# A two-layer feed-forward behind a short convolution, on one core: from the 37th group of tokens on, first-layer matmuls of 512 columns that two groups share

## The chip, the core and the metric

One NeuronCore of a Trainium2 chip runs the whole program. Its engines are TensorE (PE, with its weight loads shown apart as PEld), VectorE (DVE), ScalarE (ACT), GpSimd (POOL) and SyncE (SP), which issues most of the transfers. Each engine takes its instructions in the order in which the program lists them. The metric is the device time of one execution in microseconds, as the median of several runs.

## The reference, cut to what matters

The input has 8 sequences of 4224 tokens with 192 features; all of it is float32. Seven weights for each token and head are made by a softmax, and each token becomes the weighted sum of itself and the six tokens before it. Then comes a layer norm, a first layer of 192 to 768 with a ReLU, and a second layer of 768 to 192 whose result is added to the layer's input.

```python
w = softmax(weight_gen)                      # (8, 4224, 8 heads, 7)
y[b, s] = sum over k of w[b, s, :, k] * x_pad[b, s + k]     # per head, 24 features each
mu, var = mean(y), mean((y - mu) ** 2)
xn = (y - mu) / sqrt(var + 1e-6) * g_ln
out = y + maximum(xn @ w_ch1, 0) @ w_ch2     # 192 -> 768 -> 192
```

## The kernel before

**Tiling.** A tile is 128 rows of tokens, 16 stretches of each of the 8 sequences; there are 264 tiles. Four tiles make a group, so there are 66 groups, and TensorE works group by group. Ahead of it, in chunks of 4 or 6 tiles, `softmax` and `conv` make `y` (DVE multiplies at L511, POOL and transfers add), and `norm` makes the normalised tokens in two halves, a high and a low float16 part, which a transfer (`turn`, L652) transposes into a buffer `xT`.

**First layer.** For each group, `products` runs three units. A unit (`unit_products`, L670) covers two of the six 128-row blocks of the hidden layer: for each block 9 terms, each with two matmuls of 64 rows, one in the upper and one in the lower half of the array, that run at the same time into two banks of a PSUM buffer `ph`. Each matmul streams the 256 columns that one group has in such a half, so a unit has 36 matmuls. There are two `ph` buffers. `evict` empties one: ACT writes the ReLU as float16 into `hh` (L685), and DVE then writes the remainder into `hlo` (L687). `hh` and `hlo` have two buffers each, one group to a buffer.

**Second layer.** `half_output` (L721) multiplies a group's hidden values with the two halves of the second weights: 72 matmuls of 192 columns, again two at a time, into the one buffer `po`. It runs twice for each group, `p0` and `p1`; between them the row halves swap banks, behind a small SP instruction called `hop`. After `p1`, `merge` adds the result to `y` on DVE (L773, `f`). The last group goes through `output` (L750).

**Order.** Nothing is scheduled by the compiler. Each operation has a name, and the table `PLACE` gives for each name and count its place in one list of 2392 operations for all engines; the program is written out in that order. So an engine's order is the list's, cut down to that engine. For TensorE it repeats `unit`, `unit`, `p0` of the group before, `unit`, `p1` of the group before. At the start the weights arrive as float64 words, and DVE, ACT and POOL turn them into float16 halves (`from_double`, `w_scale`, `weights`); `w_scale` has a tiny matmul in it (L860), once for each layer. A `wake` (L642) of 11 matmuls comes right before the first unit.

Of the kernel before, what the change touches and what calls it, by code (L numbers as in the profile page):

```python
# [16 lines left out]
P = 128  # L17
ALPHA = 8.0
NT = 4
# [6 lines left out]
HALF = 512  # L26
TINY = struct.unpack("<f", struct.pack("<I", (1023 - 126) << 20))[0]
# [4 lines left out]
    'wload': (3, 9, 33, 42, 82, 86, 121, 257, 191, 373, 568, 527, 770, 1053, 851, 1068, 1156, 1216, 1427, 1301,  # L32
        1465, 1705, 1809),
    'load': (26, 12, 32, 37, 85, 87, 102, 103, 84, 120, 298, 261, 337, 260, 421, 466, 456, 526, 338, 569, 642,
        641, 756, 712, 769, 783, 849, 885, 978, 1067, 979, 1162, 1159, 1163, 1302, 1343, 1368, 1369, 1572, 1426,
        1566, 1569, 1613, 1806, 1768, 1769, 1808, 1938, 1905, 2076, 2134, 2035),
    'w_load': (40, 11, 13, 0, 1, 2),
    'w_load2': (58,),
    'w_as': (67,),
    'w_av': (41, 44, 65, 73),  # L40
    'w_an': (80,),
    'w_cs': (20,),
    'w_cv': (15, 17, 22, 23),
    'w_cn': (45,),
    'w_s1': (81, 88, 97, 104, 112),
    'w_h': (122, 123, 125, 127),
    'w_l': (153, 156),
    'w_m': (190, 193, 195, 192),
    'w_c2s': (71, 124, 146),
    'w_c2v': (72, 74, 76, 78, 91, 105, 130, 135, 137, 139, 161, 163),  # L50
    'w_c2n': (93, 144, 168),
    'w_s2': (169, 171, 182, 184, 212, 206, 207, 213),
    'max': (4, 10, 34, 43, 89, 136, 138, 352, 234, 446, 665, 608, 868, 1070, 935, 1103, 1258, 1261, 1474, 1430,
        1592, 1712, 1837),
    'sub': (5, 18, 51, 110, 111, 203, 320, 431, 551, 653, 750, 844, 967, 1148, 1090, 1243, 1406, 1441, 1581,
        1684, 1812, 1850, 1947),
    'exp': (6, 19, 52, 115, 114, 227, 321, 436, 552, 659, 751, 860, 983, 1166, 1114, 1255, 1418, 1459, 1582,
        1700, 1825, 1875, 1964),
    'sum': (7, 21, 66, 131, 133, 242, 350, 495, 553, 664, 752, 929, 1009, 1168, 1126, 1260, 1431, 1480, 1591,
        1719, 1834, 1907, 1991),  # L60
    'rcp': (8, 25, 70, 141, 175, 293, 384, 505, 573, 689, 802, 930, 1011, 1170, 1197, 1289, 1501, 1500, 1628,
        1720, 1880, 1960, 2043),
    'inv': (14, 29, 77, 162, 221, 324, 471, 545, 655, 746, 879, 947, 1078, 1202, 1259, 1388, 1536, 1540, 1644,
        1754, 1928, 2006, 2044),
    'mul': (16, 31, 90, 185, 315, 416, 525, 639, 742, 831, 933, 1018, 1128, 1231, 1328, 1433, 1537, 1636, 1738,
        1823, 1930, 2039, 2131),
    'keep': (24, 54),
# [16 lines left out]
    'copy': (53, 94, 126),  # L84
    'sums': (55, 57, 96, 99, 142, 140, 176, 177, 244, 246, 247, 255, 291, 295, 332, 326, 367, 396, 401, 397,
# [7 lines left out]
    'squares': (56, 68, 98, 100, 148, 147, 178, 180, 245, 251, 252, 256, 296, 306, 334, 333, 386, 398, 409, 412,  # L93
# [909 lines left out]
```

## Time and profile before

| | us |
|---|---|
| median of 3 runs | 868.77 |
| lowest and highest | 868.34, 869.21 |
| the profiled execution, first to last instruction | 867.2 |
| busy: PE, DVE, ACT, POOL | 823.4, 772.1, 683.7, 679.6 |

The span is the time between the first and the last instruction of one profiled execution; the run's time also holds what lies around it, 1.6 us by the median. Busy time is the time in which an engine has at least one instruction running; two matmuls that run at once count once. In a view of stretches, each row is a piece of the span; in a view in order of time, a bracket at the end of a row gives the idle time before the instruction and what ended it. The chain that ended last is followed back from the last instruction, at each step to what released it.

### The profile page before, as it was taken

What the parts mean: (1) busy time and instruction counts of PE and PEld (TensorE: products, weight loads), DVE (VectorE), ACT (ScalarE), POOL (GpSimd) and SP (SyncE); (2) the same over time, 40 slices, a digit from 0 to 9 for tenths busy, and PEclk for the clock granted to TensorE, in tenths of its full rate; (3) what the DMA queues carried; (4) which work ended last, traced back from release to release, by engine and by line L of the source; (5) the groups of instructions that cost most, each with busy time, mean ns of one, the idle gap of its engine ahead of it and who ended that gap; (6) DMA issues with size and microseconds to landing.
All of it is one profiled execution on the core that took longest, in us unless ns stands there. A gap on an engine that the chain in (4) does not pass through costs nothing.

```text
span 867.2 us, 37431 instructions
## 1 busy us (share of the span) xinstructions
PE 823.4 (95%) x16665; PEld 787.7 (91%) x16665; DVE 772.1 (89%) x796; ACT 683.7 (79%) x1781; POOL 679.6 (78%) x390
## 2 busy tenths in 40 slices
PE   3857999999999999999999999999999999999997
PEld 2526999999999999999999999999989999999997
DVE  6899999999999999999999999999989989874442
ACT  2798898799678889889888789787887888796631
POOL 3399999899889999897887889888976788885100
PEclk9968999999999999999999999999999999999999
DMA  7768868988897958988899698878948569565123
GB/s 193 190 127 166 166 163 184 200 176 180 194 193 151 220 94 188 213 181 180 160 205 195 149 213 175 165 139 187 207 99 200 120 151 190 124 127 106 40 76 110
DMA packets 137465, 140.89 MB, mean 162 GB/s; under 512 B 107479, under 2 KB 109015, under 8 KB 137303
## 3 DMA queue, kind: packets, MB, share of 16 engines
q1 hardware_dynamic: 123175, 88.95, 44.9%
q0 software_dynamic: 13824, 49.55, 29.6%
q8 instruction: 130, 2.13, 1.1%
q14 instruction: 32, 0.26, 0.1%
q10 hardware_dynamic: 304, 0.00, 0.0%
HBM read 36.43 MB, written 25.95 MB: 72 GB/s over the span
## 4 chain that ended last, share of the span: by engine, by line
PE 68%; DVE 9%; issue 2%; DVEq 0%
PE ph L670 34%; PE po L721 34%; DVE pr L511 4%; DVE hlo L687 2%; DVE y L511 1%; DVE y L773 1%; PE ph L750 1%; DVE sm L449 0%; DVE mx L440 0%; DVE wn L465 0%; DVE wn L460 0%; DVE wn L461 0%; DVE wn L459 0%; DVE wn L599 0%; DVE wn L601 0%
## 5 line engine op out<-in xcount | busy, mean ns | idle before, releaser
L514 POOL TENSOR_TENSOR y<-y,pr 128x1152 f32<-128x1152 f32 (+1 forms) x192 | 474.5, 2499 | 39.0 <-DVE pr L511 22.1
L670 PE MATMUL ph<-xT,c_w 64*128 64x256 f16 x7128 | 420.0, 270 | 10.5 <-DVE hlo L687 7.8
L670 PEld LDWEIGHTS <-c_w 64*128 64x128 f16 x7128 | 377.6, 94 | 28.3 <-issue 13.5
L721 PE MATMUL po<-c_w2h,hh 64*128 64x192 f16 x3120 | 392.5, 243 | 1.4 <-issue 1.0
L721 PE MATMUL po<-c_w2h,hlo 64*128 64x192 f16 x3120 | 392.4, 243 | 0.5 <-issue 0.5
L721 PE MATMUL po<-c_w2l,hh 64*128 64x192 f16 x3120 | 392.4, 243 | 0.0
L721 PEld LDWEIGHTS <-hh 64*128 64x128 f16 x6240 | 345.7, 94 | 2.8 <-issue 1.9
L511 DVE TENSOR_TENSOR pr<-x,wn 128x2304 f32<-128x2304 f32 (+1 forms) x150 | 332.5, 2226 | 6.6 <-POOL y L514 1.8
L687 DVE SCALAR_TENSOR_TENSOR hlo<-ph,hh 128x1024 f16<-128x1024 f32 x198 | 239.2, 1219 | 57.2 <-ACT hh L685 56.9
L685 ACT ACTIVATE hh<-ph 128x1024 f16<-128x1024 f32 x198 | 200.3, 1015 | 105.2 <-PE ph L670 101.7
L721 PEld LDWEIGHTS <-hlo 64*128 64x128 f16 x3120 | 225.5, 94 | 0.7 <-issue 0.7
L648 POOL TENSOR_TENSOR hl<-xh,hl 128x768 f16<-128x768 f32 x66 | 115.0, 1748 | 44.5 <-ACT hl L635 33.0
L615 ACT ACTIVATE xh<-y,s 128x192 f32<-128x192 f32 x264 | 125.5, 535 | 16.1 <-DVE s L603 12.5
L569 ACT ACTIVATE junk<-y,s 128x192 f32<-128x192 f32 x264 | 119.6, 453 | 6.9
L517 POOL DMA_DIRECT2D pr<-pr x96 | 94.4, 1082 | 37.3 <-DMA xT<-hl 14.2
L564 ACT ACTIVATE junk<-y 128x192 f32<-128x192 f32 x264 | 95.1, 360 | 13.6 <-POOL y L514 7.2
L773 DVE SCALAR_TENSOR_TENSOR y<-po,c_fs,y 128x768 f32<-128x768 f32 (+1 forms) x80 | 67.9, 860 | 5.4 <-PE po L721 5.4
L511 DVE TENSOR_TENSOR y<-x,wn 128x1152 f32<-128x1152 f32 (+1 forms) x51 | 60.0, 1181 | 0.1
L635 ACT ACTIVATE hl<-xh 128x768 f16<-128x768 f32 x66 | 55.0, 837 | 2.1 <-DMA xT<-hl 1.1
L564 ACT ACTIVATION_READ_ACCUMULATOR junk<-y 128x1 f32 x264 | 49.5, 188 | 0.0
L569 ACT ACTIVATION_READ_ACCUMULATOR junk<-y,s 128x1 f32 x264 | 49.4, 187 | 0.0
L532 PE MATMUL ph<-pr,ident 128*128 128x384 f32 x72 | 27.1, 531 | 16.5 <-DVE pr L511 15.6
(76 smaller groups left out, 298.5 us busy)
## 6 DMA issues: line engine op xcount, KB each, us to landing
pr<-pr POOLq DMA_DIRECT2D x60, 576.0 KB, 7.8
x<-in_x_dram SPq DMA_DIRECT2D x30, 576.0 KB, 6.3
out_dram<-y SPq DMA_DIRECT2D x30, 576.0 KB, 5.2
pr<-pr POOLq DMA_DIRECT2D x36, 384.0 KB, 5.8
x<-in_x_dram SPq DMA_DIRECT2D x20, 384.0 KB, 5.5
out_dram<-y SPq DMA_DIRECT2D x20, 384.0 KB, 5.3
w<-in_weight_gen_dram SPq DMA_DIRECT2D x21, 336.0 KB, 5.8
pr<-in_moe_w_ch_dram SPq DMA_DIRECT2D x1, 1152.0 KB
```

Source lines behind the costliest of these rows:

```text
L511: E.tensor_tensor(out=ov, in0=xv, in1=wv, op=ALU.mult)
L514: Q.tensor_tensor(out=flat(0), in0=flat(0), in1=flat(k), op=ALU.add)
L517: return Q.dma_start(flat(to), flat(k), accum_op=ALU.add, max_dma_last_dim=CHUNK * D * 4)
L564: A.activation(junk, at(y)[:, j, :], AF.Identity, scale=-1.0 / D, accum_out=at(s4)[:, 3, t : t + 1])
L569: A.activation(junk, at(y)[:, j, :], AF.Square, bias=at(s4)[:, 3, t : t + 1], accum_out=at(s4)[:, 0, t : t + 1])
L615: A.activation(paired(xh, t), at(y)[:, i, :].rearrange("p (c q) -> p c q", q=P // 2), AF.Identity, bias=at(s4)[:, 3, g + t : g + t + 1], s ...
L648: lambda xh=xh, hl=hl: Q.tensor_tensor(out=halves(hl, True), in0=pairs(xh), in1=halves(hl, False), op=ALU.subtract),
L670: T_.matmul(ph[:, r, v * 2 * P : (v + 1) * 2 * P], W["w1"][rows, WB[r][c], w, f : f + P], xv[rows, a, c, :, :], start=(v == 0 and k == 0), ...
L685: lambda: A.activation(at(hh)[:, us, :], at(ph), AF.Relu), [ph], [(hh, u)])
L687: lambda: V.scalar_tensor_tensor(out=at(hlo)[:, us, :], in0=at(ph), scalar=0.0, in1=at(hh)[:, us, :], op0=ALU.max, op1=ALU.subtract),
L721: made.append(T_.matmul(at(po)[:, z, e * D : (e + 1) * D], token(b, 2 * z + e, j)[rows], W[w][rows, j, :], start=(ph == 0 and e == 0 and k ...
L773: V.scalar_tensor_tensor(out=ysl, in0=at(po)[:, zs[0] : zs[-1] + 1, : 2 * D], scalar=W["fs"][:, 0:1], in1=ysl, op0=ALU.mult, op1=ALU.add)
```

## The change

- Pairs 18 to 31 of groups (the 37th to the 64th group) take a new path, `wide_unit`. Six wide units do the first layer of a pair: each covers one 128-row block for both groups, with 18 matmuls of 512 columns, where before a pair had six units of 36 matmuls of 256 columns. The other 38 groups keep the narrow units.
- `xT` becomes two buffers of a pair each (before: three of a group). `hh` and `hlo` become one tile each with three interleaved slots a, b and c: even groups use a, odd groups b and c in turn.
- A wide unit is evicted as before, with 1024 elements per row on ACT and on DVE. The sixth one of a pair is evicted in two halves of 512, one for each group.
- TensorE's order for a wide pair: `q0` and `q1` (the first half of the second layer of the pair before's even group, cut into hidden blocks 0 to 4 and 5), wide unit 0, `p1` of that group, wide unit 1, half of `p0` of the odd group, wide unit 2, the other half, wide unit 3, half of `p1`, wide unit 4, the other half, wide unit 5. So one second-layer piece stands between any two wide units.
- The constants `ones` and `ident` move into the space of the second weights, and the float64 words and their float32 forms into `xT` and two slots of `hlo`; the accesses there become rows of 128.
- The table `PLACE` is new for all 2460 operations, those of the start and of the narrow groups too. In it `wake` has place 135 (before 208), the first three units have 176, 195 and 217 (before 209, 210 and 224), the second layer's tiny matmul stands behind the first unit (184; before 169 and ahead of `wake`), and the load of the second weights has place 25, ahead of the load of `x` for the third chunk at 26 (before 58 and 37).

```diff
+NARROW = 18
 PLACE = {
...
+    'q1': (1561, 1616, 1706, 1774, 1841, 1920, 1983, 2047, 2128, 2194, 2258, 2320, 2371, 2417),
...
-    pool("xT", 3, [P, NT * NB, P], F16)
-    pool("hh", 2, [P, NF, NT * P], F16)
-    pool("hlo", 2, [P, NF, NT * P], F16)
+    pool("xT", 2, [P, 2 * NT * NB, P], F16)
+    HID = {q: cp.tile([P, 2 * NF, 3, 2 * P], F16, name=q) for q in ("hh", "hlo")}
+    for q in HID:
+        for i, m in enumerate("bac"):
+            plan.pools[q + m] = [HID[q][:, :, i, :]]
...
+    W = {k: cp.tile([P, NF, D], F16, name="c_" + k) for k in ("w2h", "w2l")}
+    ones, ident = (W[k].rearrange("p j d -> p (j d)").bitcast(F32)[:, :P] for k in ("w2h", "w2l"))
...
-            xh, hl, xT = Buf("xh"), Buf("hl"), Buf("xT")
+            xh, hl = Buf("xh"), Buf("hl")
+            m = (S0 + g) // NT
+            if m % 2 == 0:
+                pairs_.append(Buf("xT"))
+            xT, h = pairs_[m // 2], m % 2 ^ m // 2 % 2
+            pa["xT"][g] = (xT, h)
...
+    def wide_products(gps, j, part):
+        xv = at(gps[0]["xT"][0]).rearrange("p (i a c) q -> p a c i q", a=2, c=NB)
+        ph = at(gps[0]["ph"][j])
+        for k, (a, w, c) in list(enumerate(terms))[part]:
+            for r, rows in enumerate((top, bot)):
+                f = (j * P + (F // 2 if r and c == 2 else 0)) % F
+                T_.matmul(ph[:, r, :], W["w1"][rows, WB[r][c], w, f : f + P], xv[rows, a, c, :, :],
+                          start=k == 0, stop=k == len(terms) - 1)
...
+    def wide_unit(gps, j):
+        if j not in gps[0]["ph"]:
+            wide_part(gps, j, "uw", 1944)
...
+        for a, b in ((0, 2),) if j < NF - 1 else ((gps[0]["xT"][1], gps[0]["xT"][1] + 1), (gps[1]["xT"][1], gps[1]["xT"][1] + 1)):
+            who = [gps[z] for z in order[a:b]]
+            n = (b - a) * 2 * NT * P // 2
+            op("ACT", a_ns(n, 50), ("relu", s), lambda a=a, b=b: A.activation(cells("hh", a, b), sums(a, b), AF.Relu), [ph],
+               [(gp["hh"], j) for gp in who])
+            op("V", v_ns(n, 6), ("hlo", s),
+               lambda a=a, b=b: V.scalar_tensor_tensor(out=cells("hlo", a, b), in0=sums(a, b), scalar=0.0, in1=cells("hh", a, b),
+                                                       op0=ALU.max, op1=ALU.subtract),
+               [ph, *((gp["hh"], j) for gp in who)], [(gp["hlo"], j) for gp in who])
...
-    def half_output(gp, ph, s):
+    def half_output(gp, ph, s, js=range(6), es=range(2)):
...
+    def split_output(gp, s):
+        for js in (range(5), range(5, NF)):
+            half_output(gp, 0, s, js)
...
-    raw = (Buf("hh"), Buf("hh"), Buf("pr"))
+    raw = (Buf("xT"), Buf("xT"), Buf("pr"))
...
-        wac, w2r = Buf("hlo"), Buf("hlo")
+        wac, w2r = Buf("hlob"), Buf("hloc")
...
+            q = "a" if m % 2 == 0 else "cb"[m // 2 % 2]
+            groups.append(dict(hh=Buf("hh" + q), hlo=Buf("hlo" + q), pa=pa, g=g, s=pa["S"] + g, m=m, xT=pa["xT"][g], ph={}))
+    for m in range(0, len(groups), 2):
+        gps = groups[m : m + 2]
+        if NARROW <= m // 2 < len(groups) // 2 - 1:
+            first = m // 2 == NARROW
+            for j in range(NF):
+                if j == 0 and not first:
+                    split_output(ahead, prev["s"])
+                wide_unit(gps, j)
+                if first:
+                    if j in (1, 3):
+                        half_output(prev, j // 2, gps[0]["s"])
+                elif j == 0:
+                    half_output(ahead, 1, prev["s"])
+                elif j < 5:
+                    half_output(prev, (j - 1) // 2, gps[0]["s"], es=((j - 1) % 2,))
+            ahead, prev = gps
+            continue
```

## Rows read from the trace of the kernel before

**Rows 1.** The page: span, and busy time of each engine.
```profile
span 867.2 us, 37431 instructions
PE 823.4 (95%) x16665; PEld 787.7 (91%) x16665; DVE 772.1 (89%) x796; ACT 683.7 (79%) x1781; POOL 679.6 (78%) x390
```

**Rows 2.** Stretches: us, busy of PE, PEld, DVE, ACT, POOL; clock; DMA share, GB/s.
```profile
0.00:12.00 12.00, 0.00 (x0) 0.00 (x0) 5.08 (x17) 4.78 (x11) 3.46 (x10) 1.00 0.74 179
12.00:72.00 60.00, 41.05 (x177) 23.94 (x178) 55.75 (x88) 44.27 (x131) 39.89 (x26) 0.87 0.73 168
82.00:500.00 418.00, 413.21 (x8767) 409.06 (x8763) 408.61 (x400) 355.97 (x942) 375.52 (x216) 1.00 0.84 179
500.00:840.00 340.00, 337.98 (x7187) 325.72 (x7185) 286.31 (x277) 267.50 (x684) 250.83 (x136) 1.00 0.68 143
```

**Rows 3.** The chain that ended last, steady state: start, us, what.
```profile
676.18 2.97 PE po L721 x72
679.15 3.93 PE ph L670 x72
683.08 2.97 PE po L721 x72
686.05 1.97 PE ph L670 x36
```

**Rows 4.** The same chain, its last piece.
```profile
856.81 6.06 PE ph L750 x72
```

**Rows 5.** PE's waits, whole span: us, times, longest.
```profile
PE po L860 <- DVE hlo L846: 10.6, 1, 10.6
PE ph L670 <- DVE hlo L687: 7.8, 7, 5.2
```

**Rows 6.** PE in order of time, 57 to 80 us.
```profile
58.15 1.44 PE L860 MATMUL po<-c_s,ones 128*128 128x1 f32 x6 [10.56 <-DVE hlo L846]
...
59.45 4.66 PE L642 MATMUL ph<-hl 128*128 128x512 f16 x11
...
64.04 4.10 PE L670 MATMUL ph<-xT,c_w 64*128 64x256 f16 x72
73.35 6.08 PE L670 MATMUL ph<-xT,c_w 64*128 64x256 f16 x72 [5.21 <-DVE hlo L687]
```

**Rows 7.** DVE in order of time: a wait, the first eviction, the sixth unit's.
```profile
36.48 1.75 DVE L511 TENSOR_TENSOR pr<-x,wn 128x1536 f32<-128x1536 f32 x1 [1.39 <-PE po L860]
...
72.08 1.22 DVE L687 SCALAR_TENSOR_TENSOR hlo<-ph,hh 128x1024 f16<-128x1024 f32 x1
...
90.04 1.22 DVE L687 SCALAR_TENSOR_TENSOR hlo<-ph,hh 128x1024 f16<-128x1024 f32 x1
```

**Rows 8.** The load of the second weights: issues, KB each.
```profile
pr<-in_moe_w_ch_dram SPq DMA_DIRECT2D x1, 1152.0 KB
```

**Rows 9.** Groups by line and shape: busy us, mean ns, idle before.
```profile
L687 DVE SCALAR_TENSOR_TENSOR hlo<-ph,hh 128x1024 f16<-128x1024 f32 x198 | 239.2, 1219 | 57.2 <-ACT hh L685 56.9
L511 DVE TENSOR_TENSOR pr<-x,wn 128x2304 f32<-128x2304 f32 x90 | 228.4, 2545 | 0.6 <-POOL y L514 0.3
...
L773 DVE SCALAR_TENSOR_TENSOR y<-po,c_fs,y 128x768 f32<-128x768 f32 x50 | 50.5, 1010 | 3.4 <-PE po L721 3.4
...
L511 DVE TENSOR_TENSOR y<-x,wn 128x1152 f32<-128x1152 f32 x30 | 40.4, 1345 | 0.1
...
L449 DVE TENSOR_REDUCE sm<-e 128x96 f32<-128x672 f32 x21 | 17.7, 844 | 0.0
L440 DVE TENSOR_REDUCE mx<-w 128x96 f32<-128x672 f32 x21 | 17.7, 843 | 0.0
L773 DVE SCALAR_TENSOR_TENSOR y<-po,c_fs,y 128x384 f32<-128x384 f32 x30 | 17.4, 610 | 2.0 <-PE po L721 2.0
```

**Rows 10.** ACT, then DVE, in order of time: one unit's eviction.
```profile
602.67 1.03 ACT L685 ACTIVATE hh<-ph 128x1024 f16<-128x1024 f32 x1 [2.13 <-PE ph L670]
...
603.73 1.23 DVE L687 SCALAR_TENSOR_TENSOR hlo<-ph,hh 128x1024 f16<-128x1024 f32 x1 [0.47 <-ACT hh L685]
```

**Rows 11.** A short stretch at the start, columns as in rows 2.
```profile
73.30:77.40 4.10, 4.05 (x40) 3.21 (x41) 3.48 (x5) 1.96 (x4) 4.10 (x3) 0.50 0.66 148
```

More of the change, by code (lines that the diff above doesn't have):

```diff
@@ new lines @@
+    'newton': (82, 124, 175, 198, 286, 291, 350, 426, 501, 575, 651, 721, 817, 919, 1015, 1107, 1199, 1312,
[13 rows of a table added]
+    'wake': (135,),
[4 rows of a table added]
+    'turn': (152, 180, 234, 214, 315, 347, 404, 399, 471, 463, 541, 546, 618, 644, 696, 682, 753, 756, 830,
[21 rows of a table added]
+    'halo': (226, 647, 868, 1205, 1426, 1721, 2169),
+    'unit': (176, 195, 217, 223, 240, 253, 267, 272, 287, 303, 318, 333, 352, 363, 367, 384, 386, 408, 423,
[6 rows of a table added]
+    'relu': (183, 200, 224, 251, 241, 258, 274, 289, 300, 307, 323, 343, 354, 370, 376, 392, 396, 416, 425,
[12 rows of a table added]
@@ L199 @@
+    'hlo': (189, 206, 228, 252, 242, 259, 282, 294, 304, 308, 325, 345, 359, 377, 381, 401, 400, 420, 429,
[16 rows of a table added]
+    'hop': (248, 279, 329, 368, 403, 444, 479, 519, 553, 589, 628, 671, 702, 740, 770, 812, 841, 874, 908,
[26 rows of a table added]
 }
@@ L687, in evict, with wide_part @@
            lambda: V.scalar_tensor_tensor(
-               out=at(hlo)[:, us, :], in0=at(ph), scalar=0.0, in1=at(hh)[:, us, :],
+               out=at(hlo)[:, us, :], in0=sums(), scalar=0.0, in1=at(hh)[:, us, :],
                op0=ALU.max, op1=ALU.subtract),
-           [ph, (hh, u)], [(hlo, u)])
+           [ph, (hh, 2 * u), (hh, 2 * u + 1)], [(hlo, 2 * u), (hlo, 2 * u + 1)])
+    def wide_part(gps, j, key, cost, part=slice(None)):
+        if j not in gps[0]["ph"]:
+            gps[0]["ph"][j] = Buf("ph")
+        s = gps[0]["s"] + j * NT / 3
+        op("PE", cost, (key, s), lambda: wide_products(gps, j, part),
+           [(gp["xT"][0], h) for h, gp in enumerate(gps)] + W1S, [gps[0]["ph"][j], "pe"], lat=420.0)
@@ new lines, in wide_unit, with cells, sums @@
+    def wide_unit(gps, j):
+        if j not in gps[0]["ph"]:
+            wide_part(gps, j, "uw", 1944)
+        else:
+            wide_part(gps, j, "ub", 1296, slice(3, None))
+        ph, s = gps[0]["ph"][j], gps[0]["s"] + j * NT / 3
+        lo = gps[0]["m"] // 2 % 2 ^ 1
+        order = sorted(range(2), key=lambda z: gps[z]["xT"][1])
+        def cells(q, a, b):
+            k = j // 2 * 4 + j % 2
+            return HID[q][:, k : k + 3 : 2, lo + a : lo + b, :].rearrange("p r h x -> p r (h x)")
+        def sums(a, b):
+            return at(ph)[:, :, a * 2 * P : b * 2 * P]
+        for a, b in ((0, 2),) if j < NF - 1 else ((gps[0]["xT"][1], gps[0]["xT"][1] + 1), (gps[1]["xT"][1], gps[1]["xT"][1] + 1)):
[7 more added lines that the diff above has]
+               [ph, *((gp["hh"], j) for gp in who)], [(gp["hlo"], j) for gp in who])
@@ L733, in hop @@
                 tc.add_manual_dep(h.ins, m.ins.name, apart, reason="row halves swap banks")
+        cost, last = 247 * len(js) * len(es), js[-1] == NF - 1 and es[-1] == 1
         if ph == 0:
-            op("PE", 2930, ("p0", s), mm, whole(gp), [(po, 0), (po, 1), "pe"], lat=360.0)
-            op("SP", 60, ("hop", s), hop, [(po, 0)], [(po, "hop")])
-        else:
-            op("PE", 2930, ("p1", s), mm, [*whole(gp), (po, "hop")], [(po, 0), (po, 1), "pe"], lat=360.0)
-            merge(gp, range(NT), s)
+            key = "q0" if js[-1] < NF - 1 else "q1" if js[0] else "p0"
+            op("PE", cost, (key, s), mm, whole(gp, js), [(po, 0), (po, 1), "pe"], lat=360.0)
+            if last:
+                op("SP", 60, ("hop", s), hop, [(po, 0)], [(po, "hop")])
+        else:
+            op("PE", cost, ("p1", s), mm, [*whole(gp, js), (po, "hop")], [(po, 0), (po, 1), "pe"], lat=360.0)
+            if last:
+                merge(gp, range(NT), s)
+    def split_output(gp, s):
+        for js in (range(5), range(5, NF)):
+            half_output(gp, 0, s, js)
     def output(gp, t, s):
@@ L939, in weights @@
            ["w2h", "fs", *wv], ["w2"])
+    pairs_ = []
     todo = list(softs)
@@ L957 @@
         norm(pa)
-    prev = None
+    groups = []
     for pa in parts:
         for g in range(0, pa["n"], NT):
-            prev = dict(hh=Buf("hh"), hlo=Buf("hlo"), pa=pa, g=g, s=pa["S"] + g, xT=pa["xT"][g], ph={}, prev=prev)
-            for u in range(3):
-                products(prev, u)
-                if u and prev["prev"]:
-                    half_output(prev["prev"], u - 1, prev["s"])
+            m = len(groups)
+            q = "a" if m % 2 == 0 else "cb"[m // 2 % 2]
+            groups.append(dict(hh=Buf("hh" + q), hlo=Buf("hlo" + q), pa=pa, g=g, s=pa["S"] + g, m=m, xT=pa["xT"][g], ph={}))
+    prev = None
+    for m in range(0, len(groups), 2):
[15 more added lines that the diff above has]
+            continue
+        if m // 2 == len(groups) // 2 - 1:
+            split_output(ahead, prev["s"])
+        for i, gp in enumerate(gps):
+            tail = i == 0 and m // 2 == len(groups) // 2 - 1
+            for u in range(3):
+                products(gp, u)
+                if tail and u == 0:
+                    half_output(ahead, 1, prev["s"])
+                elif u and prev:
+                    half_output(prev, u - 1, gp["s"])
+            prev = gp
     for t in range(NT):
```

155 lines of the change are left out of this document (74 added, 81 removed), and 245 rows, old and new, of the table PLACE.

## Prediction

> **What bounds the kernel now.** I read the page first: PE is busy for 823 of 867.2 us, DVE for 772 [rows 1]. A share over the whole span says little here, so the stretches came next. Up to 82 us PE often waits (busy for 41.05 of the 60 us from 12 to 72); from 82 to 500 us it is idle for only 418.00 - 413.21 = 4.8 us, and from 500 to 840 us for 2.0 us [rows 2]. DVE is almost as full in the first of these (idle 9.4 us) and has room in the second (idle 53.7 us) [rows 2]. So there are two stages to judge: a start, in which the first units wait for others, and a long stage in which PE sets the pace. The chain that ended last agrees: in the steady state it is PE alone, 2.97 + 3.93 + 2.97 + 1.97 = 11.84 us for a group, without a gap [rows 3], and it ends with PE's last group at 862.9 us, behind which only a merge and the last store come [rows 4]. PE's list of waits shows what is left to win by order alone: 10.6 us before the second layer's tiny matmul and 7.8 us on evictions, of which 5.2 are one wait at 73.35 us [rows 5, 6].
>
> **Part 1, the longer matmuls.** Two units are 72 matmuls of 256 columns, two at a time, in 3.93 us: 109.2 ns for such a couple. A second-layer half is 36 couples of 192 columns in 2.97 us: 82.5 ns [rows 3]. The difference of 64 columns costs 26.7 ns, or 0.417 ns per column; 256 columns are then 106.8 ns, and 2.4 ns of a couple don't depend on its length. No row shows a couple of 512 columns at this clock. From below: nothing is saved, 2 x 109.2 = 218.4 ns. From above: all that doesn't depend on length is gone twice, 213.6 ns. Near the line through the two rows, with one fixed part left, it is 213.6 + 2.4 = 216.0 ns, and I take that. A wide pair has 54 couples in place of 108, so 14 pairs save 14 x 54 x 2.4 = 756 x 2.4 ns = 1.8 us; the bounds are 0 and 3.6 us. The 1512 weight loads that go were not on the path: PEld is idle for 14.3 us from 500 to 840 us, against PE's 2.0 [rows 2].
>
> The Trainium skill (TensorE: Matmul & The Clock Gate, "Wait — 56ns, not 53.3ns?") gives 215.7 ns for 512 columns at 2.4 GHz; by that figure the saving would be 756 x 2.7 ns = 2.0 us, and no run before shows it.
>
> **Part 2, the evictions.** A wide unit leaves 1024 elements per row as before, at 1.03 us on ACT and 1.22 us on DVE [rows 9, 10]. The sixth of a pair is cut in two, which adds the fixed part of one instruction on each engine, 14 times. The two merge shapes bound that on DVE: one of 768 elements takes 1.01 us and one of 384 takes 0.61, so a cut costs 0.21 us [rows 9]. That is 14 x 0.21 = 2.9 us on DVE, and I take the same for ACT, where no row shows such a cut; it is hidden in DVE's 53.7 us and ACT's 72.5 us of idle time in that stretch [rows 2], and would cost 2.9 us without that cover.
>
> **Part 3, less room between PE's pieces.** Before, a merge could take 3.93 us, since two units stand between `p1` and the next `p0` [rows 3]. In a wide pair one unit of 54 couples / 6 = 9 x 216.0 = 1.94 us stands there. A merge needs 1.01 us if DVE is free [rows 9], but DVE takes it in order, behind what the list puts ahead. The tightest place is the end of a pair: wide unit 4, 1.48 us of `p1`, wide unit 5, then `q0`, which needs `po` free. That is 1.48 + 1.94 = 3.42 us for the eviction of unit 4 and the merge. A free eviction shows at 602.67: ACT starts, DVE ends at 603.73 + 1.23 = 604.96, so 2.29 us [rows 10]; with a merge of 1.01 behind it, 3.30 us. It fits by 0.1 us. For the narrow groups there were 6.9 us of room between a group's last unit and the `p0` that reads it (2.97 + 3.93). From below a wide pair waits for nothing; from above it waits behind one convolution multiply, 2.54 us [rows 9], so 14 x 2.54 = 35.6 us. I take what the stretch shows now, 2.0 us for all of it [rows 2], so no change: where the list puts a merge or eviction right behind the matmul that feeds it, PE's order around it repeats, and DVE has 53.7 us to give. Queued behind a late merge on DVE are the next eviction and the convolution; PE waits for the merge through `po` and for the eviction through `ph`.
>
> Ahead of the first wide eviction the new list puts four more multiplies of 2.54 us on DVE and one of 1.35 and three reductions of 0.84 fewer, so 6.3 us more [rows 9]. DVE's idle time from 82 to 500 us, 9.4 us, covers it [rows 2]; without that cover it would come out as up to 6.3 us of PE's time, once.
>
> **Part 4, the start.** In the list before, PE has the second layer's tiny matmul and `wake` ahead of its first unit. The matmul starts at 58.15 after 10.6 us of idle time, `wake` at 59.45, the first unit at 64.04 [rows 5, 6]. In the new list the first unit is behind neither wait, so it can start up to 64.04 - 58.15 = 5.9 us earlier if its weights and tokens are there. But the first unit's gain is not PE's: units three and four start at 73.35 because of DVE's eviction [rows 6, 7]. I counted DVE's operations in both lists. Ahead of the first eviction there are 63 instead of 72; ahead of the sixth unit's there are the same 85. So from there on DVE arrives as before, unless it waits less on the way. It waits 60.00 - 55.75 = 4.25 us from 12 to 72 us [rows 2], of which 1.39 are one wait for PE's first tiny matmul [rows 7]. The gain is at most 4.3 us. The loss: the second weights' 1152 KB now pass the third chunk's tokens on SP's queue [rows 8], and at 179 GB/s as in the first 12 us [rows 2] that is up to 6.6 us later for that chunk's multiplies, less what DVE has to do meanwhile. The early `wake` may leave the clock down for the first units; it stood at 0.50, the level of 1.2 GHz, from 73.3 us, behind the 5.2 us wait, and there two units took 6.08 us and not 3.93 [rows 6, 11]. DVE hides that as well. Between -4.3 and +6.6 I take -0.5: the wait on the first tiny matmul is the likeliest to shrink, and the list of 85 is the same.
>
> **Parts at nothing.** The new `xT`, the moved constants and the accesses in rows of 128 change no operation's count or size; DVE and ACT work on the weights ends before 82 us, so their cost would show in the start, and is inside its bounds. `hop` has one unit between `p0` and `p1` as before (1.94 for 1.97 us); it is an instruction behind transfers on SP's queue, and a wait there would hold PE. The end of the list after the 64th group has the same pieces.
>
> **Sum.** The profiled execution is 867.2 us by span and the median of the runs 868.77, 1.56 us more. Span: 867.2 - 1.8 - 0.5 = 864.9; time: 866.5 us.
>
> **Rivals.** A. The forecast: parts 1 and 4 as taken, 865.0 to 868.0 by the saving's bounds and a little of the start. Chance 0.45.
>
> B. The start gives DVE's 4.3 us: 868.8 - 1.8 - 4.3 = 862.7, or 863.5 with part of it. For it: no tiny matmul ahead of the first unit. Against it: the 85 operations. Chance 0.16.
>
> C. Nothing comes out: waits of 0.13 us per wide pair use up the 1.8 us, or a couple of 512 columns costs two of 256. 868.8 us. For it: 0.1 us of room in part 3. Chance 0.19.
>
> D. Slower: the merge at a wide pair's end comes late. If it starts behind half an eviction, 0.6 us, at each pair, 14 x 0.6 = 8.4 us are lost: 868.8 - 1.8 + 8.4 = 875.4. It decides from (1.8 + 1.7) / 14 = 0.25 us per pair on. For it: one unit where two stood. Against it: DVE is idle for 16% of that stretch [rows 2]. Chance 0.16.
>
> E. A much larger fixed part per matmul, which shorter ones pay and longer ones don't. At 24 ns, ten times what the rows give, 756 couples fewer would save 18.1 us: 850.7. Both rows lie on a line that leaves 2.4 ns [rows 3], so chance 0.02. The Trainium skill (TensorEngine Tiling (Array Packing), "Instruction Overhead") states about 60 cycles per matmul, which is about that size as an estimate; this trace disagrees with it for matmuls that follow each other.
>
> F. The clock falls in the wide stage, because PE pauses more often. One fall costs 6.08 - 3.93 = 2.15 us for two units [rows 3, 6]; at every pair, 14 x 2.15 = 30 us: 897. The granted clock is 1.00 from 82 to 840 us, across the waits there [rows 2]. Chance 0.02. The Trainium skill (TensorE: Matmul & The Clock Gate, "A second HAM failure mode: psum-queue depth-cycling") describes that for matmuls of 512 columns that cycle through PSUM.
>
> **How the numbers follow.** What a measurement here tells from no change is about 0.2%, 1.7 us: faster means under 867.0. A gives 0.29 faster and 0.16 same; with B and E faster is 0.47; with C same is 0.35; D and F make slower 0.18. The range goes from 863.0, which leaves out E and the full gain of B (0.05 together), to 871.5, which leaves out most of D and F (0.15). A's own range is 865.0 to 868.0.
>
> **What would show it.** Right: matmuls of 512 columns at 216 ns per couple, a wide pair's period of 23.5 us and not 23.7, PE idle by about 2 us in the wide stage. Part 4: the sixth unit's eviction ends near 90.04 + 1.22 = 91.3 us, as before [rows 7]. Wrong: PE waits on `y` (L773's successor) or on `hlo` ahead of `q0`, or a granted clock under 1.00 there, or a start that differs by more than 2 us.

## The result and the profile after

The changed kernel takes 876.05 us (median of 4 runs, 874.95 to 877.62), the kernel before 868.56 us beside it. The ratio is 1.0087, with a 95% interval of 1.0072 to 1.0103: slower by 0.9%, where a gain of 0.3% was forecast, and outside the range of 863.0 to 871.5. The profiled execution after has a span of 873.2 us and a time of 874.95 us, so 6.0 us of span more than before [rows 1]; it is the fastest of the four, and the medians lie 7.5 us apart. A ratio here and below is taken over the fast runs beside the kernel before and need not be the quotient of two medians, and it leaves out three slow runs of two of the kernels below (1249.55 to 3074.32 us).

The page after: span, busy times, and the shares of the chain that ended last; then the chain's shares on the page before.

```profile
span 873.2 us, 34411 instructions
...
PE 826.1 (95%) x15153; PEld 717.6 (82%) x15153; DVE 774.2 (89%) x810; ACT 685.1 (78%) x1795; POOL 679.4 (78%) x390
...
PE 45%; DVE 33%; POOL 7%; issue 6%; ACT 6%; DMA 2%; SPq 1%; DVEq 0%; POOLq 0%
```

```profile
PE 68%; DVE 9%; issue 2%; DVEq 0%
```

In the steady state before, the chain was PE alone [rows 3]. Over the whole span DVE had 9% of it, and now it has 33%: PE is waiting for others, and the stretches say where (columns as in rows 2).

```profile
12.00:72.00 60.00, 45.51 (x233) 28.94 (x235) 57.22 (x89) 46.61 (x136) 41.04 (x26) 0.90 0.71 172
82.00:500.00 418.00, 410.12 (x8685) 402.87 (x8682) 409.68 (x399) 356.32 (x943) 378.13 (x217) 1.00 0.84 181
500.00:840.00 340.00, 335.26 (x5608) 252.03 (x5605) 282.86 (x290) 266.96 (x697) 247.00 (x134) 1.00 0.67 143
```

Up to 72 us PE is busier than before, by 4.5 us. From 82 to 500 us it is idle for 7.9 us and not 4.8, and from 500 to 840 us for 4.7 and not 2.0 [rows 2]. The granted clock is 1.00 in both, so it is not the clock. PE's list of waits, whole span (us, times, longest), names what it waits for:

```profile
PE ph L699 <- DVE hlo L720: 12.2, 11, 3.6
PE ph L699 <- ACT junk L582: 5.9, 1, 5.9
PE po L786 <- DVE y L847: 4.5, 7, 1.5
...
PE po L786 <- SPq L797: 1.1, 2, 0.7
PE ph L688 <- DVE hlo L754: 1.1, 1, 1.1
PE ph L688 <- DMA xT<-hl: 0.6, 2, 0.4
```

Before, evictions had 7.8 us of PE's time and the tiny second-layer matmul 10.6 [rows 5]; merges had 0.3 us in one place, and `hop` and the transposes none. Now the merges, L847, have 4.5 us in seven places, and `hop` (L797) and the transposes are on the list.

A pair in the wide stage in which no long wait falls looks as forecast. The chain that ended last, late in the stage:

```profile
807.48 1.94 PE ph L688 x18
809.42 3.02 PE po L786 x72
812.43 1.94 PE ph L688 x18
...
833.00 3.04 PE po L786 x69
```

Nine couples of 512 columns take 1.94 us, 215.8 ns each, and the pair's period is 833.00 - 809.42 = 23.58 us. The Trainium skill (TensorE: Matmul & The Clock Gate, "Wait — 56ns, not 53.3ns?") gives 215.7 ns for such a matmul at 2.4 GHz; the trace agrees.

**Three stretches.** To compare kernels I take from each trace when PE starts its 1st and 7th narrow unit, the unit that opens the 37th group, and the first narrow unit of the last pair of groups. With a wide stage one second-layer half, 2.97 us, is still to be done at that last point, and is added to the third stretch. All in us:

```
                           1st unit  7th unit  7th to 37th group  37th group to last pair
before                       64.04     89.61         409.21              334.16
after                        55.24     89.36         412.46              337.11
old_order_new_buffers        65.02     93.87         407.60              333.73
new_order_then_narrow        56.72     90.91         413.21              335.00
old_order_then_wide          64.85     93.77         415.23              337.27
wide_matmuls_cut             55.70     89.86         412.73              339.78
wide_waits_moved             56.71     90.93         412.76              333.64
old_order_own_w2             64.14     89.11         408.04              333.69
old_order_own_w2_again       63.84     88.72         409.19              332.10
after_own_w2                 55.17     91.29         413.12              337.18
own_w2_waits_moved           56.29     92.89         412.94              334.31
after_own_w2_mended          56.20     90.09         413.22              337.14
old_order_wide_moved         64.63     89.43         409.87              332.29
old_order_wide_moved_cut     64.11     89.03         409.64              336.45
narrow_waits_moved           54.84     89.04         412.18              334.17
```

After against before: -0.25 at the 7th unit, +3.25 up to the 37th group, +2.95 in the wide stage, which is the 6.0 us of span. The first column moves by up to 1.9 us between executions of the same order (54.84 to 56.72), so a difference of 1 us in a single trace is read from the stretches and not from the end.

### The profile page after: what moved, and what is told of

It is laid out like the page before. It is cut to its first block, busy times and chain, and to the rows that moved or that the text cites. A ratio compares the mean times of both kernels' runs of the same rounds, so it can differ in the third digit from the quotient of the medians.

```text
span 873.2 us, 34411 instructions
## 1 busy us (share of the span) xinstructions
PE 826.1 (95%) x15153; PEld 717.6 (82%) x15153; DVE 774.2 (89%) x810; ACT 685.1 (78%) x1795; POOL 679.4 (78%) x390
## 3 DMA queue, kind: packets, MB, share of 16 engines
q8 instruction: 118, 1.93, 0.9%
## 4 chain that ended last, share of the span: by engine, by line
PE 45%; DVE 33%; POOL 7%; issue 6%; ACT 6%; DMA 2%; SPq 1%; DVEq 0%; POOLq 0%
PE po L786 21%; DVE pr L524 15%; PE ph L688 12%; PE ph L699 9%; DVE hlo L720 6%; POOL y L527 5%; DVE y L847 3%; DVE y L524 2%; ACT junk L582 2%; PE ph L545 1%; DVE hlo L754 1%; ACT junk L577 1%; DMA xT<-hl 1%; ACT hh L751 1%; DMA x<-in_x_dram 1%
## 5 line engine op out<-in xcount | busy, mean ns | idle before, releaser
L527 POOL TENSOR_TENSOR y<-y,pr 128x1152 f32<-128x1152 f32 (+1 forms) x192 | 465.7, 2432 | 39.3 <-DVE pr L524 16.6
L786 PEld LDWEIGHTS <-hh 64*128 64x128 f16 x6240 | 304.8, 94 | 26.7 <-issue 9.2
L699 PE MATMUL ph<-xT,c_w 64*128 64x256 f16 x4104 | 245.0, 273 | 18.4 <-DVE hlo L720 12.2
L699 PEld LDWEIGHTS <-c_w 64*128 64x128 f16 x4104 | 221.4, 95 | 28.0 <-issue 14.5
L688 PE MATMUL ph<-xT,c_w 64*128 64x512 f16 x1512 | 177.5, 376 | 1.7 <-DVE hlo L754 1.1
L786 PEld LDWEIGHTS <-hlo 64*128 64x128 f16 x3120 | 172.6, 94 | 0.6 <-DVE hlo L754 0.6
L718 ACT ACTIVATE hh<-ph 128x1024 f16<-128x1024 f32 x114 | 115.3, 1013 | 63.6 <-PE ph L699 60.2
L720 DVE SCALAR_TENSOR_TENSOR hlo<-ph,hh 128x1024 f16<-128x1024 f32 x114 | 138.1, 1218 | 16.4 <-ACT hh L718 14.5
L754 DVE SCALAR_TENSOR_TENSOR hlo<-ph,hh 128x1024 f16<-128x1024 f32 (+1 forms) x98 | 104.7, 1068 | 39.1 <-ACT hh L751 38.5
L688 PEld LDWEIGHTS <-c_w 64*128 64x128 f16 x1512 | 81.1, 94 | 64.9 <-issue 1.2
L751 ACT ACTIVATE hh<-ph 128x1024 f16<-128x1024 f32 (+1 forms) x98 | 87.2, 894 | 57.6 <-PE ph L688 41.1
L577 ACT ACTIVATE junk<-y 128x192 f32<-128x192 f32 x264 | 95.1, 360 | 10.6 <-POOL y L527 3.9
L847 DVE SCALAR_TENSOR_TENSOR y<-po,c_fs,y 128x768 f32<-128x768 f32 (+1 forms) x80 | 67.7, 860 | 14.8 <-PE po L786 14.7
```

What stands on the lines that cost most here:

```text
L527: Q.tensor_tensor(out=flat(0), in0=flat(0), in1=flat(k), op=ALU.add)
L577: A.activation(junk, at(y)[:, j, :], AF.Identity, scale=-1.0 / D, accum_out=at(s4)[:, 3, t : t + 1])
L688: T_.matmul(ph[:, r, :], W["w1"][rows, WB[r][c], w, f : f + P], xv[rows, a, c, :, :], start=k == 0, stop=k == len(terms) - 1)
L699: T_.matmul(ph[:, r, v * 2 * P : (v + 1) * 2 * P], W["w1"][rows, WB[r][c], w, f : f + P], xv[rows, a, c, :, :], start=(v == 0 and k == 0), ...
L718: lambda: A.activation(at(hh)[:, us, :], sums(), AF.Relu), [ph], [(hh, 2 * u), (hh, 2 * u + 1)])
L720: lambda: V.scalar_tensor_tensor(out=at(hlo)[:, us, :], in0=sums(), scalar=0.0, in1=at(hh)[:, us, :], op0=ALU.max, op1=ALU.subtract),
```

## The experiments

My theory after the traces: half the loss is the new order of the narrow groups, half are waits in the wide stage; the longer matmuls save what was forecast, and the buffers cost nothing. Rivals: the buffers and their strides; the long matmuls themselves; one of the two halves alone.

**Old order, new buffers.** All groups narrow, PLACE of the kernel before, everything else as changed but for two conditions that let the last pair take the narrow path:

```diff
-NARROW = 18
+NARROW = 33
-    'unit': (176, 195, 217, 223, ...
+    'unit': (209, 210, 224, 228, ...
```

> All groups narrow, in the order of the kernel before (one transpose of 2392 operations is moved by six places, since the paired buffer is free only then), but with the changed kernel's buffers: paired xT, interleaved first-layer buffers read with strides, constants laid over other tiles. Theory (the loss is half in the new order of the start and the narrow groups, half in waits of the wide stage, and buffers cost nothing): 868.6 us, as before, within 1 us. Rival, layout (strided accesses and shared buffers cost the time): slower, by 3 us or more, up to the whole 7.5 us, so 871.5 to 876.

Measured: 871.26 us, ratio 1.0024 (1.0016 to 1.0033). Neither: 2 us slower by the ratio, all from the start, where the third unit comes at 77.37 us and not at 73.35 [rows 6]. PE, DVE and GpSimd of this kernel in order of time:

```profile
77.37 2.96 PE L692 MATMUL ph<-xT,c_w 64*128 64x256 f16 x26 [7.86 <-DVE hlo L713]
...
76.09 1.23 DVE L713 SCALAR_TENSOR_TENSOR hlo<-ph,hh 128x1024 f16<-128x1024 f32 x1 [3.15 <-ACT hl L645]
...
73.10 2.96 POOL L1006 TENSOR_TENSOR c_w2l<-hlo,c_w2h 128x1152 f16<-128x1152 f32 x1
```

The first eviction (L713) stands idle for 3.15 us; the row names an operation of ACT, but it carries a wait on GpSimd's semaphore too, and it starts when GpSimd's L1006 ends, at 73.10 + 2.96 = 76.06. L1006 reads the float32 copy of the second weights. In the changed layout that copy lies in one third of the interleaved `hlo` tile, and the eviction writes another third of it. No cell is shared, but the one waits for the other. From the 7th unit on this kernel is no slower than before (407.60 and 333.73).

**That wait taken away.** The copy goes into a `y` buffer; with it one convolution step that needs such a buffer (`c2` of the ninth chunk, 0.95 us) moves from ahead of the first eviction to behind the second:

```diff
-        wac, w2r = Buf("hlob"), Buf("hloc")
+        wac, w2r = Buf("hlob"), Buf("y")
...
-            if b is not w2r:
-                b, o = b[0], o + (F if b[1] == "c" else 0)
+            if b is w2r:
+                return rows_of(at(b).rearrange("p t d -> p (t d)")[:, o : o + n])
+            b, o = b[0], o + (F if b[1] == "c" else 0)
```

> All groups narrow in the order of the kernel before and with the new buffers, as in old_order_new_buffers, but the float32 copy of the second weight lies in a buffer of its own kind (a y buffer) and no longer in a third of the interleaved tile that the first evictions write; one convolution step (c2 of the ninth chunk) stands behind the second eviction instead of ahead of the first. Theory (the 4.0 us that old_order_new_buffers lost between its second and third unit were the first eviction waiting for GpSimd to have read that copy): third unit 3 to 4 us earlier, total 868.6 to 869.5 us. Rival (strided accesses slow the start): third unit as late as there, 871 us.

> old_order_own_w2 once more, on the chip of these three, so that the wide stage of old_order_wide_moved can be set against the narrow one from the same start: 867 us, a ratio of 0.997 to 1.000 to the kernel before.

Measured: 866.88 us, ratio 0.9991 (0.9975 to 1.0006), and the second time 867.20 us, 0.9992 (0.9983 to 1.0000). PE, DVE and GpSimd of the first:

```profile
72.76 7.42 PE L692 MATMUL ph<-xT,c_w 64*128 64x256 f16 x86 [4.51 <-DVE hlo L713]
...
71.48 1.22 DVE L713 SCALAR_TENSOR_TENSOR hlo<-ph,hh 128x1024 f16<-128x1024 f32 x1
...
73.69 1.23 DVE L713 SCALAR_TENSOR_TENSOR hlo<-ph,hh 128x1024 f16<-128x1024 f32 x1 [0.21 <-ACT hh L711]
...
72.42 2.98 POOL L1007 TENSOR_TENSOR c_w2l<-y,c_w2h 128x1152 f16<-128x1152 f32 x1
```

The second eviction now runs while GpSimd reads the copy (72.42 to 75.40), the first starts before that, and the third unit comes 4.6 us earlier. The moved convolution step has a part in this: against the kernel before, where nothing waits for the copy, the third unit comes 0.6 us earlier (72.76 for 73.35), so about 4.0 us are the shared tile's. Strides, paired `xT` and moved constants cost nothing that can be measured.

**The two halves, spliced.** New order to the 37th group and old narrow order from there, and the reverse:

```diff
-order: the new list, 2460 operations
+new_order_then_narrow: the new list up to the first wide unit, then what is left, in the old list's order
+old_order_then_wide: the old list's first 1427 operations, then what is left, in the new list's order
```

> The changed kernel's buffers and its order up to the first wide unit; from there all groups stay narrow, in the order of the kernel before. Theory: the first wide unit came 3.0 us later in the trace of after than of before, and nothing makes that good later: 868.6 + 3.0 = 871.6 us. Rival, wide stage alone (what is late by then is taken back where PE has room): 868.6 us. Rival, order of the start alone (all the loss is in the new order): 876 us.

> The changed kernel, but its first 1427 operations stand in the order of the kernel before; the rest, with all wide units, in its own. Theory: 876.05 - 3.0 = 873.0 us, still slower than before by 4.5 us. Rival, order of the start alone: 868.6 - 1.8 = 866.8 us, the forecast gain of the longer matmuls. Rival, wide stage alone: 876 us.

Measured: 877.78 us, 1.0112 (1.0086 to 1.0137), and 880.84 us, 1.0138 (1.0122 to 1.0154). Both missed. A splice has a price of its own: where one list takes over, what is in hand does not fit it. In the first, PE has one wait of 2.7 us for a merge behind the passage, at 510.88 us; its six runs go from 875.15, the one profiled, to 882.79 us, and that spread stays unexplained. In the second, PE's waits from 82 to 503 us show the price,

```profile
PE ph L695 <- DVE hlo L716: 6.1, 6, 4.1
```

with one of 4.1 us by the passage, at 495.51 us; its second stretch is 415.23 us, against 407.60 for the same order without the splice. Away from the passage they say what the theory wants: with the new order the second stretch is 413.21, and the wide stage behind the old order takes 337.27, as in the changed kernel.

**The long matmuls cut in two.**

```diff
-                T_.matmul(ph[:, r, :], W["w1"][rows, WB[r][c], w, f : f + P], xv[rows, a, c, :, :],
-                          start=k == 0, stop=k == len(terms) - 1)
+                for v in range(2):
+                    T_.matmul(ph[:, r, v * 2 * P : (v + 1) * 2 * P], W["w1"][rows, WB[r][c], w, f : f + P],
+                              xv[rows, a, c, 2 * v : 2 * v + 2, :], start=k == 0 and v == 0,
+                              stop=k == len(terms) - 1 and v == 1)
```

> The changed kernel with each matmul of 512 columns cut into two of 256; order, buffers and evictions stay. Theory: 756 couples of 215.8 ns become pairs of couples at 2 x 109.2 = 218.4 ns, 2.0 us in all, less where PE then waits less: 876.9 to 878.1 us. Rival (the long matmul is itself the loss, its result being late by one more half): faster than 876 us.

Measured: 879.40 us, 1.0146 (1.0118 to 1.0175), 3.4 us more than the changed kernel by the medians, and over the expected 2.0. In the third stretch it is 339.78 - 337.11 = 2.7 us. PE's waits there hold two pauses without a releaser, 1.4 and 0.7 us, that the changed kernel's don't, and 1.3 us less of merges and `hop`, so the 2.7 us are not the matmuls' alone. The direction is settled, as the two intervals don't touch: the long matmuls save.

**The waits of the wide stage moved.** 17 operations change places, each by a few; nothing else does:

```diff
 SP, twice:        -turn 40, hop 37        +hop 37, turn 40
 DVE, eight times: -hlo 140, f 52          +f 52, hlo 140      (a merge ahead of an eviction)
 DVE, five times:  -c3 42, hlo 144         +hlo 144, c3 42     (a convolution step and an eviction or step)
 ACT, twice:       -relu 170, squares 119  +squares 119, relu 170
```

> The changed kernel with 17 of its 2460 operations moved a few places in the order of the wide stage: two transposes behind the hop that they held up, merges and evictions ahead of the convolution step that stood before them on VectorE or ScalarE. Nothing else differs. Theory (the 4.8 us of waits on TensorE in the wide stage come from where single operations stand, not from the wide form): 2.5 to 3.5 us faster than the changed kernel, 872.5 to 873.5 us. Rival (with one unit of room the wide form has these waits in any order; they reappear at the next operation): within 1 us of 876 us.

Measured: 873.26 us, 1.0054 (1.0036 to 1.0071). The theory holds: 2.8 us less than the changed kernel, and in the third stretch 337.11 - 333.64 = 3.5 us. The same moves in another pair of kernels below (after_own_w2, own_w2_waits_moved) give 2.5 us by the medians and 337.18 - 334.31 = 2.9 us in that stretch. PE's waits from 503 to 840 us, first of the changed kernel, then of this one:

```profile
PE po L786 <- DVE y L847: 1.8, 4, 0.9
PE po L786 <- SPq L797: 1.1, 2, 0.7
PE ph L688 <- DVE hlo L754: 1.1, 1, 1.1
PE ph L688 <- DMA xT<-hl: 0.6, 2, 0.4
PE po L786 <- DVE hlo L754: 0.2, 1, 0.2
```

```profile
PE ph L684 <- DVE hlo L750: 1.1, 1, 1.1
PE ph L684 <- DMA xT<-hl: 0.8, 2, 0.4
PE po L782 <- DVE hlo L750: 0.2, 1, 0.2
PE po L782 <- DVE y L843: 0.2, 1, 0.2
```

Merges fell from 1.8 to 0.2 us, and `hop` is gone. How `hop` got there shows in the chain of the changed kernel:

```profile
525.79 0.42 SPq L669
526.21 0.05 issue
526.26 0.02 SPq L797
526.27 0.04 issue
526.32 3.14 PE po L786 x72
```

`hop`, an instruction that does nothing but carry an order from one half to the next, stood on SP's queue behind a transpose (L669), and PE waited 0.71 us for it. SP in order of time, and all 66 transposes (shortest, median and longest, in ns):

```profile
523.21 3.00 SPq L669 DMA_TRANSPOSE xT<-hl  x1
...
L669 SPq DMA_TRANSPOSE xT<-hl x66: 1385/1424/4017, 51.6 to 838.8; - x66
```

The transpose was issued when GpSimd's residue was done, at 523.2 us, and its issue then took 3.00 us, where the median is 1.42; the one behind the second wait, at 739.99 us, took 3.23. Why these two took so long no run shows.

**The second weights' copy, in the changed kernel.** Its third eviction has the same wait on GpSimd. DVE, then GpSimd:

```profile
76.27 1.22 DVE L720 SCALAR_TENSOR_TENSOR hlo<-ph,hh 128x1024 f16<-128x1024 f32 x1 [1.93 <-POOL c_w2l L1013]
...
73.88 2.36 POOL L1013 TENSOR_TENSOR c_w2l<-hlo,c_w2h 128x1152 f16<-128x1152 f32 x1
```

> The changed kernel with the same move of the second weight's copy into a y buffer, and no other difference. Theory: the third eviction no longer waits 1.3 us for GpSimd, so the fourth unit comes about 1.3 us earlier; part of that is lost again at the next wait: 874.8 to 876 us. Rival (the start of the narrow groups has no weight for the end): 876 us.

> The changed kernel with both edits: the second weight's copy in a y buffer, and the 17 operations of the wide stage moved. Theory: both gains add, 876 - 3 - 1 = 872 us, still slower than before by 3 us, which is the new order of the narrow groups. Rival (the waits reappear): 875 us.

> after_own_w2, with the convolution step that had to wait for the y buffer (c2 of the ninth chunk) placed behind the third eviction instead of ahead of it. Theory (after_own_w2 was slow because that step stood in VectorE's queue and waited for the buffer in place of the eviction): the fifth unit comes 1 us or more earlier than in the changed kernel and the time is 874.5 to 875.5 us. Rival: 878 us as in after_own_w2.

Measured: 878.24 us, 1.0114 (1.0096 to 1.0132); 875.77 us, 1.0088 (1.0068 to 1.0108); mended 877.02 us, 1.0102 (1.0083 to 1.0122). All three missed. In the first two a convolution step that needs that `y` buffer stands ahead of the eviction and waits in its place, longer than the eviction did (3.55 us for 1.93):

```profile
76.24 0.95 DVE L520 TENSOR_TENSOR y<-x,wn 128x768 f32<-128x768 f32 x1 [3.55 <-POOL c_w2l L1010]
...
77.88 1.21 DVE L716 SCALAR_TENSOR_TENSOR hlo<-ph,hh 128x1024 f16<-128x1024 f32 x1
```

Mended, the third eviction no longer waits for GpSimd, and the fifth unit comes 21.08 us behind the first instead of 22.31, 1.2 us earlier as expected, but the seventh only 0.2 us earlier: the next waits take it back. So this wait is real, and worth nothing that shows in the new order.

**Old order, then wide, with the waits moved.** 1342 operations in the old order with the copy in the `y` buffer, then the list of wide_waits_moved, with six more moves around the change of lists and behind it. A second kernel is the same with each long matmul made into two (the diff of wide_matmuls_cut).

```diff
-order: the new list
+order: the old list's first 1342 operations, then what is left, in the order of wide_waits_moved
-turn 45, turn 44 ... d1 32, d0 32 ... c3 44, hlo 158
+turn 44, turn 45 ... d0 32, d1 32 ... hlo 158, c3 44
```

> The first 1342 operations as in old_order_own_w2 (order of the kernel before, second weight's copy in a y buffer), the rest in the order of wide_waits_moved, with six more operations moved a few places around the passage and in the wide stage. So: old order up to the 37th group, wide form from there, no false wait at the start, few waits in the wide stage. Theory (the wide form itself is worth its 1.9 us of matmul time, and all the loss was in orders): 1 to 2 us faster than old_order_own_w2, about 865.5 us, faster than both given kernels. Rival (the wide stage keeps about as many waits as it saves matmul time): level with old_order_own_w2, 867 us. Rival (the passage from one order to the other costs as it did in old_order_then_wide, 6 us): 872 us.

> old_order_wide_moved with each matmul of 512 columns cut into two of 256; nothing else differs. Theory: with few waits left, nearly all of 756 x (2 x 109.2 - 215.8) ns = 2.0 us is added. Rival (the waits, not the matmuls, set the wide stage): under 0.7 us is added.

Measured: 868.04 us, 1.0003 (0.9995 to 1.0012), and cut 870.76 us, 1.0031 (1.0019 to 1.0043). The passage now costs little (409.87). The theory's gain did not come: by the time the first rival holds, level with old_order_own_w2. The wide stage took 332.29 us, and the narrow one of that kernel 332.10 in one execution and 333.69 in the other, which has a pause of 1.1 us without a releaser that the first has not. So the wide stage is level or up to 1.4 us ahead. It still has waits of its own, from 500 to 838 us:

```profile
PE ph L684 <- DVE hlo L750: 0.6, 1, 0.6
PE ph L684 <- DMA xT<-hl: 0.5, 1, 0.5
PE po L782 <- DVE hlo L750: 0.2, 1, 0.2
```

Against that, the narrow list of old_order_own_w2_again has there a single pause of 0.5 us. Cutting the matmuls costs 2.7 us by the medians and 336.45 - 332.29 = 4.2 us in the third stretch: the 2.0 of the theory, and in the traced execution two further pauses (1.4 us on `hop`, 0.7 without a releaser).

**The narrow groups.** In the 30 us behind the seventh unit the new order loses most of what it loses in the second stretch. Shown are the changed kernel, old_order_own_w2_again, and narrow_waits_moved, which is wide_waits_moved with five more operations moved on DVE there:

```diff
-c1 9, inv 5 ... hlo 9, f 1 ... hlo 10, sum 6 ... c3 9, hlo 11 ... c1 11, hlo 13
+inv 5, c1 9 ... f 1, hlo 9 ... sum 6, hlo 10 ... hlo 11, c3 9 ... hlo 13, c1 11
```

The stretch from 90 to 120 us in each (columns as in rows 2):

```profile
90.00:120.00 30.00, 26.70 (x554) 26.12 (x552) 27.29 (x38) 26.36 (x80) 27.50 (x20) 1.00 0.76 163
```

```profile
90.00:120.00 30.00, 29.08 (x620) 28.87 (x618) 29.22 (x41) 26.00 (x71) 29.70 (x21) 1.00 0.77 170
```

```profile
90.00:120.00 30.00, 27.31 (x570) 26.89 (x568) 27.84 (x39) 26.92 (x81) 27.46 (x19) 1.00 0.75 161
```

> wide_waits_moved with five more operations moved on VectorE between the seventh and the fifteenth narrow unit: a merge ahead of the eviction in front of it, two evictions ahead of convolution steps, two softmax steps. Theory (the 3.8 us of waits that every kernel with the new order shows in the 30 us behind the seventh unit, against 1.2 with the old order, come from single places too): 1.0 to 1.7 us less than wide_waits_moved, 871.6 to 872.3 us. Rival (VectorE is full there, so the waits come back at the next evictions): within 0.5 us of 873.3 us.

Measured: 871.57 us, 1.0041 (1.0027 to 1.0054). The median is the theory's, but its trace says less: the second stretch is 412.18 us after 412.76, 0.6 us, and the traced execution starts 1.9 us earlier by the seventh unit and loses 0.5 us in the third. So five moves take back a fifth of the 3 us, and neither side is right. In the changed kernel DVE itself is idle there for 2.7 of 30 us, 1.6 of them waiting for ACT ahead of three evictions; two of these, and the merge behind:

```profile
103.28 1.22 DVE L720 SCALAR_TENSOR_TENSOR hlo<-ph,hh 128x1024 f16<-128x1024 f32 x1 [0.56 <-ACT hh L718]
104.42 0.85 DVE L478 TENSOR_TENSOR wn<-e,wn 128x672 f32<-128x672 f32 x1
105.94 1.23 DVE L720 SCALAR_TENSOR_TENSOR hlo<-ph,hh 128x1024 f16<-128x1024 f32 x1 [0.67 <-ACT hh L718]
107.08 1.01 DVE L847 SCALAR_TENSOR_TENSOR y<-po,c_fs,y 128x768 f32<-128x768 f32 x1
```

The merge at 107.08 is what PE's `p0` waits 1.5 us for. Which of the new list's other places bring this about is not shown.

## Why the prediction was wrong, step by step

The forecast took 2.3 us off the span; 6.0 came on. Of these -0.25 us lie ahead of the seventh unit, +3.25 between it and the 37th group, and in the wide stage -2.0 of matmul time and +5.0 of pauses.

**Part 1, the longer matmuls: right.** 215.8 ns per couple for 216.0; by matmul lengths 756 x (218.4 - 215.8) = 2.0 us for 1.8. Cutting them cost 3.4 us by the medians and 2.7 in the third stretch in one pair of kernels, 2.7 and 4.2 in the other, pauses included. As an estimate, the about 60 cycles per matmul of the Trainium skill (TensorEngine Tiling (Array Packing), "Instruction Overhead"), 25 ns at 2.4 GHz, would have made it 756 x 25 ns = 18.9 us; the cut kernels disagree.

**Part 2, the split eviction: right.** Groups by shape after:

```profile
L754 DVE SCALAR_TENSOR_TENSOR hlo<-ph,hh 128x512 f16<-128x512 f32 x28 | 19.3, 688 | 10.8 <-ACT hh L751 10.5
...
L751 ACT ACTIVATE hh<-ph 128x512 f16<-128x512 f32 x28 | 16.3, 590 | 14.6 <-PE ph L688 8.7 <-DVE hlo L754 5.4 <-DVE wn L610 0.6
```

A cut costs 2 x 688 - 1219 = 157 ns on DVE, for 210. What I had not seen is the 5.4 us: the second half on ACT waits for DVE to have read the first half, again cells of one tile that don't overlap; that this is the reason is argued from the code here, as no run took it away.

**Part 3, no change in the waits: this is the step that failed in the wide stage.** I wrote that it fits by 0.1 us and that PE's order repeats, and took the 2.0 us that the stretch showed. By matmul lengths the stage has 84 x 1.942 + 56 x 2.97 = 329.4 us of work after and 331.4 before; it took 337.11 and 334.16. So 7.7 us of pauses instead of 2.7: 5.0 us more, against 2.0 saved. (The rows of the stretch show 4.7 us idle after and 2.0 before, as a matmul's end is drawn some 0.18 us into the next piece and hides that much of each wait.) An engine's average room doesn't say where single operations stand: DVE was idle for 57 us of the 340, and still merges came late, behind an eviction or a convolution step. That the places of single operations cause most of it is shown by wide_waits_moved, which takes 3.5 of the 5.0 us away.

**Part 4, the start: right as far as I counted, and I stopped too early.** The first unit starts 8.8 us earlier, past my bound of 5.9, which left out that the tiny matmul's own wait of 10.6 us goes too; nothing is left of it at the seventh, as argued. The early `wake` did not keep the clock up, as I had feared: the granted clock was 1.00 from 46 to 50 us, PE then sat idle for 5.95 us, and from 55 to 60 us it was 0.50, the level of 1.2 GHz, where the kernel before had 1.00 for its first units:

```profile
55.00:60.00 5.00, 4.76 (x40) 3.80 (x40) 4.58 (x11) 4.71 (x22) 4.63 (x4) 0.50 0.46 106
```

The first unit took 4.0 us there, for 2.0 before, and nothing of that is left at the seventh either. That the seventh unit agrees within 0.3 us is partly luck: executions of this order have it at 89.04 to 90.93 us. The sixth eviction, forecast for 91.3 us, ends at 90.92:

```profile
89.70 1.22 DVE L720 SCALAR_TENSOR_TENSOR hlo<-ph,hh 128x1024 f16<-128x1024 f32 x1
```

But the new list goes on for 102 more narrow units, and for them I put nothing into the sum: there I took only "the list of 85 is the same" and, in Part 3, a cover of 9.4 us of idle time on DVE for 6.3 us of more work. This is the second step that failed, by 3.25 us, most of it in the next 30 us. From 90 us to the 37th group PE's waits for evictions went from 2.3 to 4.5 us and those for merges from 0.3 to 2.7, while 2.1 us of pauses without a releaser that the trace before has there are gone. The cover itself held: from 120 to 500 us DVE is busy for 3.2 us more (374.55 for 371.39), and PE idle for only 0.5 us more (4.30 for 3.77).

**Parts at nothing: two were not.** `hop` behind a transpose cost 1.1 us (I named the danger and gave it no price), and the second weights' place in the `hlo` tile cost 4 us at the third unit in the old order (2 us in the time), and nothing that shows in the new.

**The rivals.** D, slower through merges at a pair's end, gave 875.4, near the time, but not by its mechanism: merges were 1.8 of 4.8 us of named waits in the wide stage, only two of these four waits, 1.1 us, stand at a pair's end, and half the loss lies ahead of the stage. Its chance should have been larger for another reason: both C and D ask what a new list does to waits, and every one of 2460 places is new. F is out, the clock stayed at 1.00 from 82 to 840 us. (Its price was a little high: 6.08 us is a row in order of time, and the same two units at 1.00 have 4.10 us in such a row [rows 6], so one fall costs 1.98 and not 2.15 us.)

## What to carry to other kernels

Where an order is written out by hand, a new list is a change of its own: price it by stretch, and expect a few us of waits from single operations standing wrong, even where each engine has idle time. A saving on the pacing engine of 2 us in 334 arrives only if nothing that feeds it is late, so look first at what the next piece waits for (here merges, an order-carrying instruction on a DMA queue, a transpose). And try the new layout with the old order and the old layout's order with the new form separately: here that showed that the layout was free but for one shared tile, and that the best version of the wide form (868.04 us) only draws level with before.

## What was not expected of the machine and its program

Operations on cells of one tile that interleave but don't overlap were ordered as if they did: 3.15 us and 1.93 us for an eviction behind GpSimd's reading, gone when the copy moved to another tile, and, as far as the code tells, 5.4 us on ACT behind DVE. A do-nothing instruction costs 0.02 us on SP, but up to 1.4 us of PE's time (in old_order_wide_moved_cut; 0.7 in the changed kernel) by what stands ahead of it. And PE sometimes pauses for up to 1.4 us with no releaser in the trace. In the old order such pauses come back near the same places (before: 420.7, 463.9, 634.5 and 671.2 us; old_order_own_w2: 462.2, 632.3 and 668.9), and the trace of the changed kernel has none behind 55 us; no run here shows why.
